# Linear attention and a gated feed-forward in one kernel: the weight fold moved to the front, output stores moved to another queue, and a new order of steps

## The chip, the cores and the metric

The kernel runs on one core of a Trainium2 chip. The metric is the device time of one execution in microseconds (us); lower is better. A core has a matrix engine (PE), a vector engine (DVE), a scalar engine (ACT), a general engine (POOL) and a synchronisation engine (SP). Each takes its instructions strictly in program order; they meet through semaphores. DMAs are issued from SP's queue (descriptors made in hardware) or POOL's (descriptors made by software), and are carried out by 16 DMA engines.

## The reference

With batch 8, 8 heads, 576 positions, head width 64, model width 512 and inner width 1024:

```python
phi = lambda x: np.where(x > 0, x, np.exp(x) - 1.0) + 1.0
q_p, k_p = phi(q), phi(k)
kv  = np.einsum('bhsd,bhse->bhde', k_p, v)
z   = np.sum(k_p, axis=2)
num = np.einsum('bhsd,bhde->bhse', q_p, kv)
den = np.einsum('bhsd,bhd->bhs', q_p, z)[..., None] + 1e-06
x   = (num / den).transpose(0, 2, 1, 3).reshape(4608, 512)
out = (((x @ w1) * (x @ w2)) @ w3) @ w_out
```

All inputs and the output are float32; the kernel multiplies in bf16 and accumulates in float32.

## The kernel before

Since `(h @ w3) @ w_out = h @ (w3 @ w_out)`, the kernel first multiplies the two weights into one, `wf` (1024 x 512): this is called the fold here. The 4608 tokens are cut into 36 tiles of 128 and 9 chunks of 512 columns. Of each batch, 512 positions make four tiles; the remaining 64 are joined with the 64 of the next batch to a ninth tile of the pair.

The whole kernel is one long list of steps, written out by hand in the string `ORDER`. A step has a letter, a batch or chunk, and a part; a `+` puts its copy on DVE instead of ACT (in a load: its DMA on POOL instead of SP). Every engine and every DMA queue does its share of the steps in this order, so a step that waits holds everything behind it on that engine or queue. The letters:

- `L`, `M`, `N`: load k, q, v of a batch (`load_qkv`; parts 0 and 1 are the halves by heads, 2 is all, 3 the 64 remaining positions). They land in a pool of five buffers (`ld`) that the raw w3 shares.
- `E0` to `E7`, `C0`, `C1`, `B0` to `B3`: load w3, w_out and the quarters of w1 and w2, on POOL's queue, with a cast from float32 to bf16 in the DMA.
- `X Y Z` for q and `x y z` for k: phi as exp (ACT), min and max (both DVE). `v`: v to bf16.
- `w`, `W`: fold of one of eight row blocks of w3. `w` is eight PE transposes and a copy, `W` eight matmuls and a copy.
- `c d e f g a b r`: attention of batch 0, with q transposed on PE (`first_tr`); `h`, `i`: the first two units of chunk 0.
- For other batches: `K` makes kv, `T` transposes q by a DMA, `A` makes numerator and denominator and divides, and x is transposed by a DMA (`D`) or on PE (`P`).
- `F c.f`: one of eight units of a chunk: 4 + 4 matmuls with w1 and w2, an ACT copy and a DVE product. `O c.m`: eight matmuls of one tile with `wf`, a copy into `o_sb`, and its store, issued in the same step: on POOL's queue, for the last chunk on SP's.

The fold's steps stand among those of chunk 0, after the attention of batch 0. The constants (identity, masks, ones) are written on POOL ahead of all steps. One explicit wait holds `B0`, and all that stands behind it on POOL's queue, until the second half of k of batch 0 has landed; another holds the load `M1.2` for `E5`.

Of the kernel before, what the change touches and what calls it, by code (L numbers as in the profile page):

```python
# [8 lines left out]
F32 = mybir.dt.float32  # L9
BF16 = mybir.dt.bfloat16  # L10
# [3 lines left out]
P = 128  # L14
NCH = 512
# [3 lines left out]
def kernel(  # L19
# [47 lines left out]


    ident = consts.tile([P, P], BF16)
    make_identity(nc, ident)  # L70

    mask = consts.tile([P, 2, 2, D], BF16)
    nc.gpsimd.memset(mask, 0.0)
    nc.gpsimd.memset(mask[0:D, :, 0, :], 1.0)
    nc.gpsimd.memset(mask[D:P, :, 1, :], 1.0)
    eps = consts.tile([P, 1], F32)
    nc.gpsimd.memset(eps, 1e-6)

    w1_sb = wpool.tile([P, KC, DFF], BF16)
    w2_sb = wpool.tile([P, KC, DFF], BF16)  # L80
# [71 lines left out]
    def copy_of(alt):  # L152
        return nc.vector.tensor_copy if alt else nc.scalar.copy
# [132 lines left out]

    kvz = {}

    def first_tr(g):
        qj, _ = ph["q", 0]  # L290
        if g == 0:
            qts[0, 0] = att.tile([P, KC, NJ * P], BF16, tag="qt", name="qt")
        tp = at_ps.tile([P, 8, P], BF16, tag="at", name="tp")
        for i in range(2):
            for j in range(NJ):
                nc.tensor.transpose(tp[:, i * NJ + j, :],
                                    qj[:, 2 * g + i, j].rearrange("p u d -> p (u d)"), ident)
# [11 lines left out]
    def first_nd(hp, own):  # L309
        if own:  # L310
            nd = [mm_ps.tile([P, 512], F32, tag="mm", name=n) for n in ("num1", "den1")]
        else:
            t = at_ps.tile([P, 2, 512], F32, tag="at", name="nd1")
            nd = [t[:, 0], t[:, 1]]
        g, a = divmod(hp, 2)
        for i, n in ((1, "z"), (0, "n")):
            nc.tensor.matmul(nd[i], kvz[n, g][:, a].rearrange("p h e -> p (h e)"),
                             qts[0, 0][:, hp], start=True, stop=True)
        r = lr.tile([P, 512], F32, tag="lr", name="lr", bufs=2)

        def recip():
            nc.scalar.activation(out=r, in_=nd[1], func=AF.Ln, bias=eps[:, 0:1])  # L322
            nc.scalar.activation(out=r, in_=r, func=AF.Exp, scale=-1.0)  # L323

        def mult():
            nc.vector.tensor_tensor(
                out=xt[:, 0:NJ, hp, :], in0=nd[0].rearrange("p (j t) -> p j t", t=P),
                in1=r.rearrange("p (j t) -> p j t", t=P), op=ALU.mult)
        return recip, mult

    def first_rest():
# [3 lines left out]
        for i, n in ((1, "z"), (0, "n")):  # L335
            for hp in range(KC):
# [1 line left out]
                nc.tensor.matmul(nd[:, i, hp * R:(hp + 1) * R],  # L338
                                 kvz[n, g][:, a].rearrange("p h e -> p (h e)"),
                                 qtr[:, a, g * R:(g + 1) * R], start=True, stop=True)  # L340
        r = lr.tile([P, 512], F32, tag="lr", name="lr", bufs=2)
        w = KC * R
        nc.scalar.activation(out=r[:, 0:w], in_=nd[:, 1, 0:w], func=AF.Ln, bias=eps[:, 0:1])
        nc.scalar.activation(out=r[:, 0:w], in_=r[:, 0:w], func=AF.Exp, scale=-1.0)
# [28 lines left out]
    def o_unit(c, m, alt=False):  # L373
        ab = abs_[c]
        o_ps = mm_ps.tile([P, DM], F32, tag="mm", name="o_ps")
        for f in range(FC):
            nc.tensor.matmul(o_ps, ab[:, f, m * P:(m + 1) * P], wf_sb[:, f, :],  # L377
                             start=(f == 0), stop=(f == FC - 1))
        o_sb = sm.tile([P, DM], F32, tag="o_sb", name="o_sb", bufs=4)
        copy_of(alt)(out=o_sb, in_=o_ps)  # L380
        kind, b, j = order[c * (NCH // P) + m]
        queue = nc.sync if c == n_chunks - 1 else nc.gpsimd
        if kind == "J":
            dst = out[b * S:b * S + NJ * P, :].rearrange("(p j) n -> p j n", j=NJ)
            queue.dma_start(out=dst[:, j, :], in_=o_sb)  # L385
        else:
            for i in range(2):
                queue.dma_start(
                    out=out[(b + i) * S + NJ * P:(b + i + 1) * S, :],
                    in_=o_sb[i * R:(i + 1) * R, :])  # L390


    WQ = 256
# [30 lines left out]
            nc.tensor.transpose(tp[:, kc, :], raw["w3", i][:, kc * P:(kc + 1) * P], ident)  # L424
# [39 lines left out]
    ctx.enter_context(tc.manual_schedule())
    src = {"k": k, "q": q, "v": v}
    held = {}
    GATE = 5

    def step(s):

# [6 lines left out]
            f_unit(b, i)  # L477
        elif t == "O":
            o_unit(b, i, alt)
        elif t == "w":  # L480
            w3_tr(b, alt)
        elif t == "W":
            wf_mm(b, alt)
        elif t in "LMN":
            name = "kqv"["LMN".index(t)]
            ins = load_qkv(name, src[name], b, i, alt)
            if b == 0:
                held[t, i] = ins
            if s == "M1.2":
                after(ins, held["E", GATE])  # L490
        elif t == "B":
            for ins in load_w12(b):
                if b == 0 and "B" not in held:
                    after(ins, held["L", 1])
                    held["B"] = True
        elif t == "C":
            load_wo(b)
        elif t == "E":
            held["E", b] = load_w3(b)
        elif t in "xX":  # L500
            phi_exp("kq"["xX".index(t)], b, i)
        elif t in "yY":
# [74 lines left out]
```

## Time and profile before

| What | Value |
|---|---|
| median of 3 runs | 267.1 us (266.4 to 267.88) |
| the profiled execution, its own time | 265.35 us |
| its span in the profile | 263.6 us |
| PE busy | 234.8 us (89%) |
| DVE / ACT / POOL busy | 165.2 / 129.4 / 42.8 us |
| moved by DMA | 50.55 MB, mean 192 GB/s |
| last PE work ends | about 258.8 us |

All positions in time below are microseconds from the start of the span. A row of a group gives the busy time, the mean time of one instruction in ns, and the idle time before them with what ended it. `SPq` is the queue on which SP issues DMAs. Matmul durations overlap their neighbours (they are pipelined), so what one costs is read from the distance of starts. L358 and the like are lines of the kernel before. The profiled execution is 1.75 us faster than the median of the runs, and its span is 1.75 us shorter than its own time.

### The profile page before, as it was taken

How to read it: one execution, taken by the hardware profiler on the slowest of the kernel's cores; microseconds unless marked ns; L12 is line 12 of the kernel's file. 1: busy time of each engine (PE TensorE's matmuls, PEld its weight loads, DVE VectorE, ACT ScalarE, POOL GpSimd, SP SyncE). 2: the span in 40 equal slices, each digit the busy share in tenths (PEclk: the TensorE clock that was granted, in tenths of full speed). 3: DMA queues.
4: the chain of work that ended last, by engine and by line, in shares of the span. 5: the costliest groups of instructions: out<-in, count | busy, mean ns of one | idle time of the engine just before them, and what ended most of it. 6: DMA issues, size and time to landing. Idle time of an engine off the chain costs nothing.

```text
span 263.6 us, 4384 instructions
## 1 busy us (share of the span) xinstructions
PE 234.8 (89%) x1591; PEld 112.2 (43%) x1608; DVE 165.2 (63%) x416; ACT 129.4 (49%) x207; POOL 42.8 (16%) x81
## 2 busy tenths in 40 slices
PE   0086999899599999995999999999999999999992
PEld 0043544454245545441544444444445444444440
DVE  0564352788668797695479886967985826442220
ACT  4465524793767693693463952624633213222211
POOL 4472500002300031030001500310110030001000
PEclk9999999999889999997999999999999999999998
DMA  6999999959999949799997994795634071011123
GB/s 234 324 180 204 212 226 321 334 111 270 281 235 269 350 139 260 224 259 277 236 338 152 216 379 95 228 160 191 145 93 133 2 178 31 20 42 50 71 88 111
DMA packets 73173, 50.55 MB, mean 192 GB/s; under 512 B 39616, under 2 KB 69312, under 8 KB 73152
## 3 DMA queue, kind: packets, MB, share of 16 engines
q1 hardware_dynamic: 63600, 35.59, 52.3%
q0 software_dynamic: 9552, 14.68, 23.7%
q8 instruction: 12, 0.20, 0.3%
q14 instruction: 9, 0.07, 0.1%
HBM read 38.80 MB, written 9.44 MB: 183 GB/s over the span
## 4 chain that ended last, share of the span: by engine, by line
PE 81%; DMA 8%; ACT 4%; DVE 3%; issue 1%; SPq 0%; POOL 0%; DVEq 0%
PE a_ps L358 25%; PE b_ps L358 24%; PE o_ps L377 19%; PE wf_ps L430 5%; DMA xt<-xn 3%; PE kvp L186 3%; DMA q32r<-in_q_dram 2%; DMA q<-in_q_dram 2%; PE nd L252 2%; PE w3p L424 1%; DVE qj L149 1%; ACT xt L273 1%; ACT o_sb L380 1%; ACT lr L322 0%; ACT lr L323 0%
## 5 line engine op out<-in xcount | busy, mean ns | idle before, releaser
L358 PEld LDWEIGHTS <-w_sb 128*128 128x128 bf16 x576 | 55.3, 99 | 69.9 <-issue 5.0
L364 DVE TENSOR_TENSOR ab<-a_sb,b_ps 128x512 bf16<-128x512 f32 x72 | 49.2, 684 | 50.4 <-PE b_ps L358 45.9
L358 PE MATMUL a_ps<-xt,w_sb 128*128 128x512 bf16 x288 | 76.8, 387 | 4.1 <-DMA xt<-xn 3.0
L363 ACT COPY a_sb<-a_ps 128x512 f32<-128x512 f32 x72 | 42.1, 586 | 73.1 <-PE a_ps L358 69.7
L358 PE MATMUL b_ps<-xt,w_sb 128*128 128x512 bf16 x288 | 76.5, 385 | 0.0
L377 PE MATMUL o_ps<-wf_sb,ab 128*128 128x512 bf16 x274 | 64.6, 379 | 1.1 <-issue 0.5
L385 POOL DMA_DIRECT2D out_dram<-o_sb x29 | 15.9, 548 | 172.9 <-ACT o_sb L380 129.6
L377 PEld LDWEIGHTS <-ab 128*128 128x128 bf16 x288 | 27.4, 98 | 31.9
L149 DVE SCALAR_TENSOR_TENSOR qj<-q,e 128x256 bf16<-128x256 f32 x64 | 23.6, 415 | 0.0
L149 DVE SCALAR_TENSOR_TENSOR kj<-k,e 128x256 bf16<-128x256 f32 x64 | 23.4, 414 | 0.1
L380 ACT COPY o_sb<-o_ps 128x512 f32<-128x512 f32 x23 | 13.4, 586 | 20.3 <-PE o_ps L377 18.3
L128 DVE TENSOR_SCALAR e<-e 128x1024 bf16<-128x1024 bf16 x32 | 13.0, 418 | 11.3 <-ACT e L124 11.3
L124 ACT ACTIVATE e<-q 128x1024 bf16<-128x1024 f32 x16 | 16.8, 1058 | 6.2 <-DMA q<-in_q_dram 6.2
L262 DVE TENSOR_TENSOR xn<-nd,r 128x512 bf16<-128x512 f32 x28 | 18.0, 685 | 0.0
L124 ACT ACTIVATE e<-k 128x1024 bf16<-128x1024 f32 x16 | 16.7, 1059 | 0.3 <-DMA k<-in_k_dram 0.3
L380 DVE COPY o_sb<-o_ps 128x512 f32<-128x512 f32 x13 | 9.0, 689 | 11.8 <-PE o_ps L377 10.8
L430 PE MATMUL wf_ps<-wo_sb,w3t 128*128 128x512 bf16 x61 | 14.6, 379 | 0.9 <-ACT w3t L425 0.7
L158 ACT CAST vt<-v 128x1024 bf16<-128x1024 f32 x14 | 14.6, 1053 | 0.8 <-DMA v<-in_v_dram 0.8
L206 PE MATMUL kvp<-vt,kj 128*128 128x130 bf16 x16 | 2.0, 264 | 13.0 <-ACT vt L158 13.0
L190 ACT COPY kvf<-kvp 128x260 f32<-128x260 f32 x14 | 5.3, 375 | 9.6 <-PE kvp L186 9.2
L430 PEld LDWEIGHTS <-w3t 128*128 128x128 bf16 x64 | 6.1, 98 | 7.8 <-ACT w3t L425 0.8
L186 PEld LDWEIGHTS <-kj 64*128 64x128 bf16 x224 | 7.1, 94 | 4.4 <-issue 3.2
(75 smaller groups left out, 157.4 us busy)
## 6 DMA issues: line engine op xcount, KB each, us to landing
out_dram<-o_sb POOLq DMA_DIRECT2D x29, 256.0 KB, 3.7
q<-in_q_dram SPq DMA_DIRECT2D x7, 1024.0 KB, 7.1
k<-in_k_dram SPq DMA_DIRECT2D x7, 1024.0 KB, 8.2
v<-in_v_dram SPq DMA_DIRECT2D x6, 1024.0 KB, 8.1
v<-in_v_dram SPq DMA_DIRECT2D x4, 512.0 KB, 7.1
w_sb<-in_moe_w_dram POOLq DMA_DIRECT2D x8, 256.0 KB, 9.0
w3b<-in_moe_w_dram POOLq DMA_DIRECT2D x8, 256.0 KB, 11.6
q<-in_q_dram SPq DMA_DIRECT2D x2, 512.0 KB, 5.1
```

What stands on the lines that cost most here:

```text
L124: nc.scalar.activation(out=e, in_=x, func=AF.Exp)
L149: nc.vector.scalar_tensor_tensor(out=out, in0=x, scalar=1.0, in1=e, op0=ALU.add, op1=ALU.max)
L158: copy_of(alt)(out=vt[:, :, 4 * i:4 * i + 4, 0:D], in_=raw["v", b].rearrange("p (h j d) -> p j h d", h=H, j=NJ)[:, :, 4 * i:4 * i + 4])
L186: nc.tensor.matmul(kvp[:, r, i * W:(i + 1) * W], kk[rows], vv[rows], start=(n == 0), stop=(n == (NJ if r == g else NJ - 1)))
L262: nc.vector.tensor_tensor(out=dst.rearrange("p (c u) e -> p u c e", u=2), in0=v4[:, :, :, 0:D], in1=r[0:n].unsqueeze(3).to_broadcast([n, 2 ...
L358: nc.tensor.matmul(ps, w[:, kc, f * P:(f + 1) * P], xt[:, 4 * c:4 * c + 4, kc, :], start=(kc == 0), stop=(kc == KC - 1))
L363: nc.scalar.copy(out=a_sb, in_=a_ps)
L364: nc.vector.tensor_mul(out=abs_[c][:, f, :], in0=a_sb, in1=b_ps)
L377: nc.tensor.matmul(o_ps, ab[:, f, m * P:(m + 1) * P], wf_sb[:, f, :], start=(f == 0), stop=(f == FC - 1))
L380: copy_of(alt)(out=o_sb, in_=o_ps)
L385: queue.dma_start(out=dst[:, j, :], in_=o_sb)
L430: nc.tensor.matmul(ps, w3ts[i][:, kc, :], wo_sb[:, kc, :], start=(kc == 0), stop=(kc == FC - 1))
```

## The change

- The list starts with `E0`, `C0`, `E1` on POOL; the constants become steps (`I`) behind them, and `w0`, `w1` are PE's first work. `U` is the first half of a fold product (w_out's first half suffices), `W` then the second. `H9` is nine matmuls on a tile of zeros.
- Explicit waits are a table: `L0.0` waits until `E0` has landed, `E4` for `N0.1`, `B0` for `L0.1`, `L1.2` for `C1`, `M1.2` for `E3`, `N1.0` for `E7`.
- All loads of q, k, v go on SP's queue (eight pairs of small ones were on POOL's).
- Stores are steps of their own (`S`), all on SP's queue; `o_sb` has five buffers instead of four.
- The last tile (`Q8.2`) is made in two column halves, one copied and stored by DVE and SP, the other by ACT and ACT's own queue. The tile with two DMAs is no longer the last.
- q of batches 1 and 2 is transposed on PE (`a`, `b`) instead of by DMA (`T`); x of batch 3 instead of batch 2 is transposed on PE (`P`), that of batch 2 by DMA (`D2.0`).
- The divisor's buffer in batch 0's attention comes from the three buffers of `a_sb`.
- The whole order is new.

```diff
     ident = consts.tile([P, P], BF16)
-    make_identity(nc, ident)
...
+    def constants(part):
+        if part == 0:
+            make_identity(nc, ident)
+        elif part == 1:
...
+        else:
+            nc.vector.memset(zero, 0.0)
+
+    def warm_up(n):
+        ps = mm_ps.tile([P, NCH], F32, tag="mm", name="warm")
+        for _ in range(n):
+            nc.tensor.matmul(ps, zero[:, 0:P], zero, start=True, stop=True)
...
-        r = lr.tile([P, 512], F32, tag="lr", name="lr", bufs=2)
+        r = sm.tile([P, NCH], F32, tag="a_sb", name="lr")
...
-        o_sb = sm.tile([P, DM], F32, tag="o_sb", name="o_sb", bufs=4)
+        o_sb = o_sbs[c, m] = sm.tile([P, DM], F32, tag="o_sb", name="o_sb", bufs=OBUF)
         copy_of(alt)(out=o_sb, in_=o_ps)
+
+    def o_store(c, m):
+        o_sb = o_sbs[c, m]
         kind, b, j = order[c * (NCH // P) + m]
-        queue = nc.sync if c == n_chunks - 1 else nc.gpsimd
...
-            queue.dma_start(out=dst[:, j, :], in_=o_sb)
+            nc.sync.dma_start(out=dst[:, j, :], in_=o_sb)
...
+    def o_last(c, m):
...
+        for i, copy, queue in ((0, nc.vector.tensor_copy, nc.sync), (1, nc.scalar.copy, nc.scalar)):
+            cols = slice(i * (DM // 2), (i + 1) * (DM // 2))
+            o_ps = mm_ps.tile([P, DM], F32, tag="mm", name="o_ps")[:, 0:DM // 2]
+            for f in range(FC):
+                nc.tensor.matmul(o_ps, ab[:, f, m * P:(m + 1) * P], wf_sb[:, f, cols],
+                                 start=(f == 0), stop=(f == FC - 1))
+            copy(out=o_sb[:, cols], in_=o_ps)
+            queue.dma_start(out=dst[:, j, cols], in_=o_sb[:, cols])
...
+        if part != 1:
+            wfs[i] = mm_ps.tile([P, DM], F32, tag="mm", name="wf_ps")
+        for kc in ((0, 1, 2, 3), (4, 5, 6, 7), range(FC))[part]:
+            nc.tensor.matmul(wfs[i], w3ts[i][:, kc, :], wo_sb[:, kc, :],
                              start=(kc == 0), stop=(kc == FC - 1))
-        copy_of(alt)(out=wf_sb[:, i, :], in_=ps)
+        if part:
+            copy_of(alt)(out=wf_sb[:, i, :], in_=wfs[i])
...
     ORDER = """
-    M0.0 L0.0 X0.0 Y0.0 M0.1 L0.3+ L0.1 x0.0 X0.1 Y0.1 N0.3 N0.0 Z0.0 v0.2 y0.0 v0.0 Z0.1 z0.0
-    Z0.2 B0 Z0.3 E0 x0.2 E1 N0.1 y0.2 x0.1 z0.1 z0.4 c0.0 a0.0 y0.1 v0.1 b0.0 z0.2 C0 d0.0 E2
...
+    L0.3 E0 I2 C0 M1.3 E1 I0 w0 L0.0 x0.2 x0.0 w1 y0.0 E2 I1 M0.0 C1 E3 y0.2 X0.0 M0.1 U0 Y0.0
+    N0.3 X0.1 Z0.0 H9 N0.0 Z0.1 Y0.1 w2+ N0.1 W0+ z0.0 N1.3 a0.0 U1 E4 E5 z0.1 b0.0 L0.1 Z0.2
+    v0.2+ W1 E6 w3 v0.0+ Z0.3 U2 z0.4 c0.0 x0.1 L1.2 X1.2 v0.1+ a0.1 d0.0 W2 E7 L1.3 b0.1 e0.0
+    y0.1 U3 w4 z0.2 B0 z0.3 f0.0 M1.2 N1.0 N1.1 Y1.2 x1.0 M2.2 c0.1 g0.0 x1.1 W3 y1.0 w5+ U4
+    e0.1 f0.1 U5 y1.1 M2.3 x1.2 d0.1 z1.0 g0.1 W4 w6 w7+ v1.2 y1.2 z1.1 W5 e0.2 X1.0 U6 Y1.0 B1
+    Z1.4 W6+ U7 Z1.0 Z1.1 f0.2 W7 g0.2 B2 e0.3 h0.0 B3 X1.1 f0.3 h0.1 z1.2 a1.0 L2.2 Y1.1 g0.3
+    Z1.2 M0.3 Z1.3 v1.0 z1.4 b1.0 h0.2 z1.3 h0.3 i0.0 K1.0 a1.1 i0.1 v1.1 L2.3 F0.2 K1.1+ b1.1
+    F0.3 L3.3 A1.0 N2.3 F0.4 X2.0 F0.5 X2.1 Y2.1 Y2.0 P1.0 A1.1 X2.2 P1.1 Y2.2 Z2.0 F0.6 N2.2
+    F0.7 T1.1 Z2.1 x2.0 X0.2 x2.1 Y0.2 Z2.4 O0.2 Z2.2 P1.3 P1.2 O0.1 y2.1 Z2.3 a2.0 y2.0 z2.0
+    z2.1 Z0.4 v2.1 x2.2 O0.0 L4.3 M3.2 b2.0+ y2.2 v2.0+ v2.2 F1.0 A1.2 z2.4 x3.2 z2.2 L3.2 F1.1
+    y3.2 F1.2 X3.0 K2.0+ X3.1 S0.1 z2.3 T0.1 Y3.0 F1.3 N3.2 S0.2 z3.4 a2.1 Z3.0 x4.2 Y3.1 b2.1
+    Z3.1 M3.3 K2.1+ F1.4 Z3.2 M4.2 x3.0 N3.3 F1.5 S0.0 Z3.3 D1.1 N4.3 x3.1 A2.0 F1.6 X3.2 F1.7
+    y4.2 O1.0 y3.0 A2.1 v3.2 z3.0 v3.1 X4.0 Y3.2 Y4.0 O1.2 z3.1 r0 z4.4 y3.1 T3.0 O1.1+ D2.0
+    Z4.0 X4.1 O1.3+ O0.3+ v3.0 Y4.1 L4.2 M5.3 M4.3 N5.3 N4.2 z3.2 z3.3 Z4.1 T2.1 L5.2 K3.0+ F2.0
+    F2.1 S1.1 K3.1+ F2.2 x4.0 Z4.2 F2.3 Z3.4 x4.1 A3.0 S1.2 F2.4 Z4.3 F2.5 X4.2 L5.3 A3.1 T3.1
+    M5.2 P3.0 F2.6 y4.0 Y4.2 P3.1+ P3.2 y4.1 Z4.4 N6.3 z4.0 X5.2 M6.3 z4.1 S0.3 F2.7 x5.0 F3.0
+    z4.2 T4.1 x5.2 v4.2+ v4.1 v4.0 S1.0 T4.0 F3.1 A3.2 x5.1 A2.2 F3.2 y5.1 O2.0 z4.3 N5.2 y5.0
+    F3.3 K4.0+ K4.1+ X5.0 L6.2 Y5.2 Y5.0 D2.1 O2.3 S1.3 z5.0 O2.2 A4.0 P3.3 F3.4 A4.1 z5.1 y5.2
+    Z5.4 F3.5 L6.3 F3.6 v5.2 X5.1 z5.2 z5.4 v5.0 Z5.0 v5.1 D3.1 Y5.1 F3.7 x6.2 x6.0 Z5.1 O2.1+
+    S2.3 D4.0 K5.0+ z5.3 x6.1 O3.1+ Z5.2 M6.2 Z5.3 S2.0 y6.0 F4.0 K5.1+ y6.1 O3.3+ F4.1 z6.0
+    S2.2 X6.0 T5.0 Y6.0 T5.1 F4.2 S3.1 X6.2 X6.1 F4.3 N6.2 Z6.0 F4.4 z6.1 Y6.2 A5.0 F4.5 F4.6
+    A5.1 y6.2 O3.2 L7.2 A4.2 F4.7 v6.0 x7.0 S2.1 v6.1 S3.3 D5.0 Y6.1 v6.2 O4.3 Z6.1 z6.4 A5.2
+    z6.2 Z6.4 S3.2 O4.0+ Z6.2 z6.3 L7.3 x7.2 y7.0 O3.0 M7.2 Z6.3 K6.0+ T6.0 F5.0 D4.1 F5.1 F5.2
+    N7.3 F5.3 N7.2 K6.1+ O4.2 X7.0 S4.3 X7.1 z7.0 A6.0 F5.4 Y7.0 F5.5 Y7.1 S3.0 x7.1 Z7.0 S4.2
+    M7.3 F5.6 D5.1 A6.1 S4.0 F5.7 v7.0 O5.1+ O4.1 Z7.1 v7.1 O5.0 O5.3 z7.1 Z7.2 X7.2 D6.0 y7.1
+    z7.2 Z7.3 y7.2 F6.0 F6.1 v7.2 z7.4 F6.2 T6.1 F6.3 A6.2 F6.4 S4.1 S5.3 T7.0 z7.3 K7.0+ S5.1
+    Y7.2 F6.5 Z7.4 K7.1+ O5.2 A7.0 F6.6 A7.1 S5.0 F6.7 O6.3 T7.1 O6.1+ A7.2 O6.2+ S5.2 D7.0 D6.1
+    O6.0 F7.0 F7.1 D7.1 F7.2 F7.3 F7.4 F7.5 F7.6 F7.7 S6.1 S6.2 O7.0+ S6.3 S7.0 F8.0 F8.1 F8.2
+    O7.2 F8.3 F8.4 F8.5 S6.0 S7.2 O7.1 S7.1 F8.6 F8.7 O7.3 O8.0 S8.0 O8.3+ S8.3 O8.1 S7.3 S8.1
+    Q8.2
     """
+    GATES = "B0<L0.1 E4<N0.1 L0.0<E0 L1.2<C1 M1.2<E3 N1.0<E7"
...
+    OBUF = 5
+
+    def loaded(s, ins):
+        s = s.rstrip("+")
+        if s in gates and gates[s] in held:
+            after(ins, held[gates[s]])
+            del gates[s]
+        held[s] = ins
```

## The prediction

> **What bounds the kernel now.** I read the page first: how much of the span is PE, and in which slices it is not.
>
> ```profile
> span 263.6 us, 4384 instructions
> PE 234.8 (89%) x1591; PEld 112.2 (43%) x1608; DVE 165.2 (63%) x416; ACT 129.4 (49%) x207; POOL 42.8 (16%) x81
> PE   0086999899599999995999999999999999999992
> DMA  6999999959999949799997994795634071011123
> PE 81%; DMA 8%; ACT 4%; DVE 3%; issue 1%; SPq 0%; POOL 0%; DVEq 0%
> ```
>
> PE carries 81% of the chain, and the slices (6.6 us each) show where it does not work: two at the start, one with 5 near 69 us, one near 122 us, and the tail. DMA is full through all of the first third. So I asked PE's waits, then the timeline at these places.
>
> ```profile
> PE kvp L206 <- ACT vt L158: 13.0, 1, 13.0
> PE a_ps L358 <- DMA xt<-xn: 3.0, 1, 3.0
> PE w3p L424 <- DVE xt L326: 1.7, 1, 1.7
> PE xtp L272 <- ACT o_sb L380: 1.6, 1, 1.6
> PE a_ps L358 <- ACT xt L273: 1.1, 1, 1.1
> ```
>
> The columns are total, times, longest. 13.0 us pass before the first matmul: q, k, v of batch 0 must land and go through phi first.
>
> ```profile
> 17.66 0.59 PE L317 MATMUL den<-qt,kvz 128*128 128x512 bf16 x1
> 18.04 0.63 PE L317 MATMUL num<-qt,kvn 128*128 128x512 bf16 x1
> 18.46 0.63 PE L317 MATMUL den<-qt,kvz 128*128 128x512 bf16 x1
> 22.07 0.38 PE L358 MATMUL b_ps<-xt,w_sb 128*128 128x512 bf16 x1
> 22.29 0.38 PE L358 MATMUL a_ps<-xt,w_sb 128*128 128x512 bf16 x1
> 69.78 1.21 PE L358 MATMUL a_ps<-xt,w_sb 128*128 128x512 bf16 x4 [1.14 <-ACT xt L273]
> 122.06 1.89 PE L358 MATMUL a_ps<-xt,w_sb 128*128 128x512 bf16 x4 [2.96 <-DMA xt<-xn]
> ```
>
> After a pause PE is slow: equal matmuls start 0.42 us apart at 18 us and 0.216 apart from 22 us. By such distances the cold start costs 2.1 us. At 69.78 the first sixteen matmuls take 5.3 us where 3.45 is normal, so 1.85 is lost; at 122.06 the first eight lose 1.66. The granted clock of the next view shows both places.
>
> ```profile
> 5.00:10.00 5.00, 0.00 (x0) 0.00 (x0) 1.20 (x4) 2.70 (x3) 0.00 (x0) 1.00 1.07 344
> 25.00:30.00 5.00, 4.49 (x37) 2.77 (x38) 2.15 (x4) 3.20 (x5) 2.26 (x4) 1.00 1.30 202
> 30.00:35.00 5.00, 5.00 (x31) 2.52 (x30) 2.42 (x5) 1.01 (x1) 1.81 (x3) 1.00 1.33 212
> 68.00:75.00 7.00, 5.85 (x29) 2.57 (x29) 3.53 (x10) 3.96 (x8) 2.10 (x4) 0.76 1.19 203
> 120.00:127.00 7.00, 4.94 (x31) 2.09 (x32) 3.50 (x10) 1.08 (x3) 0.54 (x1) 0.76 1.09 264
> ```
>
> The last three columns are clock, DMA share and GB/s. Plain loads run at 344 GB/s; while weights are cast it is about 207, counted in the bf16 bytes written, since the share is above 1 in both. These two rates price the new start.
>
> **The start.** PE's work is the same; what counts is how much of it is done by when. A fold block is eight transposes (0.45 us, from the starts 36.18 and 36.63) and eight matmuls at 0.216 (1.72): 17.4 us for eight. The attention of batch 0 before the first `h` is 4.2 us (`c` 1.6, `a` 0.9, `e` eight matmuls, 1.7). So 21.6 us of PE work stand before `h0.0` in the new order; `H9` is extra.
>
> When can it be done? w3 and w_out write 3.15 MB at 0.207 MB per us, 15.2 us; q, k, v of batch 0 without q's rest are 3.4 MB at 0.344, 9.9 us. First bytes flow at 2.3 us, so all that is in by 27.4, and by 30.5 if `L1.2` (1.05 MB, 3.05 us), free to go after `C1`, gets ahead. PE's queue has `w7` before `W5 e0.2 U6 W6 U7 W7 e0.3`: after E7 lands, 0.45 + 5.1 = 5.6 us remain. So `h0.0` starts near 36.1; its `B0` (0.52 MB, 2.5 us) is in by 33. The ends: 33.0 with E7 at 27.4; 41 if each POOL DMA lands as slowly as the median w3 row below, E7 then being in near 35.
>
> ```profile
> out_dram<-o_sb POOLq DMA_DIRECT2D x29, 256.0 KB, 3.7
> w3b<-in_moe_w_dram POOLq DMA_DIRECT2D x8, 256.0 KB, 11.6
> ```
>
> From `h0.0` to `F1.0` the new list has `h` 3.45, six F units 10.35, `a1` and `a2.0` 1.35, `K1` 1.2, `A1.0 A1.1` 0.85, eight transposes per pair of `P` 1.8 and three O units 5.2: 24.2 us, and I add 1.5 for waits like those that stand there now (0.7 on w3t, 1.1 on xt), bounds 0 to 4. `F1.0` starts near 61.8, against 69.8 now. Then it still owes `O0.3` and `A1.2` (2.0 us), which are done by now in the old order, so the lead is 6.0 us; `a2.1` takes 0.45 of it. If PE comes there without a pause, the 1.85 us of slow clock go too: 7.4. Bounds by the ends above: 11 and 0.
>
> `H9` is nine matmuls, 3.8 us at the cold distance. It stands between `U0` and `w2`, while E2 and C1 are still landing (C1 is the fourth or fifth transfer, at the rates above near 13 us), so it is in a wait and costs nothing; if they were in, it would cost 1.9 to 3.8, within the bound. What it buys is uncertain: the Trainium skill, TensorE: Matmul & The Clock Gate, section on the clock gate, says that the fast clock needs about 3.4 us of activity and is lost after an idle window as long; the trace shows the slow distance but not the window. By that rule a wait of that length behind `H9` makes the next matmuls cold again, at up to 2 us.
>
> The constants move behind three POOL DMAs. `ident` is needed by `w0`; three issues at 0.55 to 0.9 and 0.5 for the identity put it at 3.3 us, ahead of E0. `L0.0` waits for E0, and on SP all of q, k, v stands behind it. E0 is alone; the nearest rows are q's first load, read 3.8 us after issue, and w3's fastest, 6.2: E0 in near 6, and the loads already pay for this in the byte sum, since POOL's DMAs fill that time.
>
> **The middle.** The 4.6 us at 122 us (3.0 wait, 1.66 clock) come from `D3.0`, 8.3 us to landing. Batch 3 now goes through PE (0.45 each, ACT or DVE 0.6) with `F2.7` between, so this stall goes. Batch 2 takes the risk: `D2.0` follows `A2.1`. DVE needs 2.5 us after its matmuls (111.19 to 113.65 in the old trace), the transfer 4.3 (median) to 8.3, thus 6.8 to 10.8; PE has `O1.2 r0 O1.1 O1.3 O0.3 K3.0` there, 7.8 us. Stall 0 to 3.0, with slow clock 4.7. I take 1: gain 3.6, bounds 0 to 4.6.
>
> **The stores.** 35 DMAs leave POOL for SP, and 16 small loads too. SP's own store issues took 0.36 us, small loads 0.63: 23 us more of SP's queue, which is not full; two `T` at some 1.6 leave. POOL is not waited for by anyone in the middle, so nothing is gained there. But a store step waits for its copy, and behind it stand loads, `T` and `D`. Behind `S0.1` waits `T0.1`, behind `S0.0` `D1.1`, behind `S1.3` and `S2.3` `D3.1` and `D4.0`. Most `S` follow their `O` by several F units (1.73 us each), which is the cover. No row shows a store ahead of a transpose. The least is 0; the most is a stall as at 122 us, 4.6, at three places, 13.8. I take 2.5, nearer to none because of that distance. The rule against the change stands in the Trainium skill, DMA: Bandwidth & Descriptors, section "Queues, rings and completion order": a DMA engine takes turns between queue rows but consumes one row in order. By it a transpose queued behind a 256 KB store would land later by the store's bytes; the trace has no such pair. At 344 GB/s that is an estimated 0.76 us each, which the sum leaves out.
>
> **The tail.** Now: last matmul 258.8, ACT copy 0.59, two issues of 0.57, landing. Then: half a copy (0.3 less), one issue (0.57 less), but sixteen half-width matmuls instead of eight with their weight loads of 98 ns each nearly bare (up to 0.3 more). I take 0.5 less, 0 to 0.9. `lr` in `a_sb`'s buffers costs nothing while no F unit needs them, and these start after `e0.3`; a fifth `o_sb` only loosens.
>
> **Sum** against the profiled execution's own 265.35: -7.4 - 3.6 + 2.5 - 0.5 = -9.0, giving 256.35; the median of the runs is 1.75 above that execution, so 258.1.
>
> **Rivals.** (a) The start is bound by bytes and software DMAs as slow as the w3 row: `h0.0` at 41, lead 1 to 2. For: 11.6 us median landing, DMA full. Against: they were queued behind 3.4 MB and each other. Time 267.1 - 1.5 - 3.6 + 2.5 - 0.5 = 264. Chance 0.2. (b) Slower: SP's in-order queue becomes the bound. Mechanism: a store waiting for its copy holds a `T` or `D` of the next batch, at the places named. Price 4.6 each with the clock loss; with the other gains of 11.5 it breaks even between two and three such stalls, and at three the time is 267.1 - 11.5 + 13.8 = 269.4, more with four (274). For: SP waits already, 44 us in all for `D`'s inputs. Against: the distance of `S` behind `O`. Chance 0.15. (c) The fast end: no new wait, `D2.0` covered: 267.1 - 9 - 4.6 - 0.5 = 253. Chance 0.2. (d) The front does not do what it says: E0 lands late, near the 12.7 us that the slowest w3 DMA took, and holds q, k, v by its gate. Every load shifts by 6, the lead is gone, and with the store cost the time is near 267. Chance 0.05.
>
> **The numbers.** The forecast gets 0.4, 258.1; with (a) and (c) that is 0.8. The range 251 to 267.5 leaves out most of (b) and a little of the fast end. A difference below about 0.5%, 1.3 us, can't be told from none. Faster: 0.8 less a little of (a), plus part of (d): 0.8; within: 0.05; slower: 0.15.
>
> **What would show it.** Right: first matmul near 6 us, `h0.0` (first a_ps) at 33 to 41, `F1.0` at 58 to 66, no row "DMA xt<-xn" above 3 us, granted clock 1.00 at F1's start, fewer than three waits of SPq for o_sb that end a PE wait. Wrong: PE idle in two or more slices after 60 us, with the chain running through SPq or an xt transposed late; or a first a_ps beyond 42 us.

## The result, and the profile after

The changed kernel takes 268.59 us (median of 12 runs, 267.33 to 270.51), the kernel before 265.75 beside it (15 runs, 261.56 to 267.88). The ratio is 1.0225, with a 95% interval of 1.0179 to 1.0271: slower, where 258.1 and "faster" were forecast, and outside the range of 251 to 267.5. Executions of one and the same kernel lie up to 7.7 us apart, with a mean granted clock between 0.97 and 1.00, and the ratios leave slow ones out, so that the ratio is 1.0225 where the two medians alone would give 1.011. Positions in a profile are therefore compared with positions in another, ratios with ratios, and the profiled execution of a kernel may lie some us beside its median.

The same lines of the page as were shown for the kernel before, in the same order:

```profile
span 267.1 us, 4436 instructions
PE 239.0 (89%) x1630; PEld 115.8 (43%) x1649; DVE 164.4 (62%) x417; ACT 133.1 (50%) x211; POOL 14.1 (5%) x30
PE   1285945999999999999999999999999999999994
DMA  7998999996969749998959695879682144021115
PE 81%; DMA 12%; ACT 2%; issue 1%; DVE 1%; SPq 0%; ACTq 0%; POOLq 0%
```

The holes that PE had near 69 and 122 us are gone, and from the eighth slice to the last but one PE is full. Apart from the tail, nearly all of its idle time now lies in the first seven slices (46.7 us). The chain's DMA share rose from 8% to 12%. PE's waits, in total us, times and longest, name what is behind it:

```profile
PE w3p L454 <- DMA w3b<-in_moe_w_dram: 10.9, 2, 5.9
PE wf_ps L464 <- ACT wf_sb L467: 6.6, 1, 6.6
PE tp L309 <- DVE qj L162: 3.9, 1, 3.9
PE kvp L223 <- DVE kr L162: 0.9, 2, 0.4
PE wf_ps L464 <- issue: 0.4, 2, 0.2
PE o_ps L390 <- issue: 0.3, 2, 0.2
```

That is the whole list. Nothing above 0.5 us comes from the middle: no transposed x is waited for, and no store. Rows of PE's timeline give the places that the prediction named, the first `a_ps` (`h0.0`) and `F1.0`, and the wait of 6.6 us ahead of them:

```profile
5.05 1.03 PE L454 MATMUL w3p<-ident,w3b 128*128 128x128 bf16 x8 [5.05 <-DMA w3b<-in_moe_w_dram]
11.98 1.03 PE L454 MATMUL w3p<-ident,w3b 128*128 128x128 bf16 x8 [5.90 <-DMA w3b<-in_moe_w_dram]
22.84 1.28 PE L309 MATMUL tp<-ident,qj 128*128 128x128 bf16 x8 [3.94 <-DVE qj L162]
42.94 3.57 PE L464 MATMUL wf_ps<-wo_sb,w3t 128*128 128x512 bf16 x8 [6.61 <-ACT wf_sb L467]
52.51 0.38 PE L371 MATMUL a_ps<-xt,w_sb 128*128 128x512 bf16 x1
77.20 1.03 PE L371 MATMUL a_ps<-xt,w_sb 128*128 128x512 bf16 x4
```

`h0.0` starts at 52.51 instead of the forecast 36.1, and `F1.0` at 77.20 instead of 61.8 (before: 69.78). From `F1.0` to the end of the span it is 189.9 us, against 193.8 before, although the new order still owes 2.45 us of work there. So everything behind `F1.0` gained and the start lost more.

The wait of 6.6 us names ACT's copy `wf_sb`. ACT's timeline shows that this copy takes 0.57 us and was not itself the trouble:

```profile
34.46 0.63 ACT L336 ACTIVATE lr<-lr 128x512 f32<-128x512 f32 x1
40.41 2.00 ACT L137 ACTIVATE e<-k 128x1024 bf16<-128x1024 f32 x2 [5.33 <-DMA k<-in_k_dram]
42.32 0.57 ACT L467 CAST wf_sb<-wf_ps 128x512 bf16<-128x512 f32 x1
```

ACT stood from 35.1 to 40.4 before `x1.0`, the exp of batch 1's k, whose load had not landed. The copy of `W3` stands behind it in the order, and PE needs the PSUM tile that this copy frees. The chain of waits says why the load was late (start, length, what):

```profile
5.49 14.96 DMA q<-in_q_dram
...
24.34 2.54 PE wf_ps L464 x7
27.35 12.98 DMA k<-in_k_dram
40.41 2.00 ACT e L137 x2
42.94 3.57 PE wf_ps L464 x8
```

Rows of the waits of POOL, and then of SP's queue, complete it, with the row of SP's timeline where the load `N1.0` is issued:

```profile
POOL w3b L445 <- DMA v<-in_v_dram: 18.8, 1, 18.8
```

```profile
SPq L120 <- PE w3p L454: 5.0, 1, 5.0
SPq L120 <- DMA w3b<-in_moe_w_dram: 3.7, 2, 2.2
```

```profile
36.01 5.67 SPq L120 DMA_DIRECT2D v<-in_v_dram  x2
```

SP's load `L1.2` takes the next of the five `ld` buffers, which the raw w3 shares; it waits 5.0 us until PE has transposed an earlier block (`w3`), and that stands in PE's queue behind `a0.0`, which waits for q of batch 0. POOL meanwhile idles 18.8 us at the gate `E4<N0.1`, until 25.4. The longest wait for w3, 2.2 us, ends at 36.0: there `N1.0` is released by its gate, so E7 has landed. From 1.2 to 13 us the DMAs are busy all the time but move only 170 GB/s; between 24 and 28 us they have little under way; and behind the 6.6 us PE runs at half clock (columns: length, busy time and count of PE, PEld, DVE, ACT, POOL, then granted clock, DMA share, GB/s):

```profile
1.20:13.00 11.80, 2.05 (x17) 1.76 (x18) 0.00 (x0) 2.15 (x3) 5.13 (x14) 1.00 1.01 170
24.00:28.00 4.00, 3.78 (x21) 1.80 (x20) 4.00 (x11) 2.10 (x3) 2.60 (x5) 0.74 0.63 151
40.00:46.00 6.00, 3.06 (x8) 1.20 (x9) 3.36 (x8) 4.00 (x6) 0.00 (x0) 0.50 1.26 247
68.00:75.00 7.00, 6.95 (x39) 3.39 (x38) 7.00 (x23) 5.64 (x11) 0.00 (x0) 1.00 1.11 355
120.00:127.00 7.00, 6.95 (x47) 3.19 (x46) 6.17 (x18) 5.69 (x9) 0.00 (x0) 1.00 0.91 172
```

The last two rows answer to the two of before that had a clock of 0.76: both are at 1.00 now.

### The profile page after: what moved, and what is told of

It reads as the page before. It is cut to its first block, busy times and chain, and to the rows that moved or that the text cites. A ratio compares the mean times of both kernels' runs of the same rounds, so it can differ in the third digit from the quotient of the medians.

```text
span 267.1 us, 4436 instructions
## 1 busy us (share of the span) xinstructions
PE 239.0 (89%) x1630; PEld 115.8 (43%) x1649; DVE 164.4 (62%) x417; ACT 133.1 (50%) x211; POOL 14.1 (5%) x30
## 4 chain that ended last, share of the span: by engine, by line
PE 81%; DMA 12%; ACT 2%; issue 1%; DVE 1%; SPq 0%; ACTq 0%; POOLq 0%
PE a_ps L371 23%; PE b_ps L371 23%; PE o_ps L390 23%; DMA q<-in_q_dram 6%; DMA k<-in_k_dram 5%; PE wf_ps L464 4%; PE kvp L199 3%; PE nd L265 2%; ACT e L137 2%; DMA w3b<-in_moe_w_dram 1%; DVE qj L162 1%; PE xtp L285 1%; PE tp L309 1%; PE o_ps L417 1%; PE w3p L454 1%
## 5 line engine op out<-in xcount | busy, mean ns | idle before, releaser
L371 PEld LDWEIGHTS <-w_sb 128*128 128x128 bf16 x576 | 54.4, 98 | 63.6 <-issue 0.4
L371 PE MATMUL a_ps<-xt,w_sb 128*128 128x512 bf16 x288 | 75.1, 380 | 0.1
L371 PE MATMUL b_ps<-xt,w_sb 128*128 128x512 bf16 x288 | 74.9, 379 | 0.0
L390 PE MATMUL o_ps<-wf_sb,ab 128*128 128x512 bf16 x264 | 63.1, 379 | 1.0 <-issue 0.3
L390 PEld LDWEIGHTS <-ab 128*128 128x128 bf16 x280 | 26.5, 98 | 30.9
L464 PE MATMUL wf_ps<-wo_sb,w3t 128*128 128x512 bf16 x61 | 18.6, 445 | 7.2 <-ACT wf_sb L467 6.6
L454 PE MATMUL w3p<-ident,w3b 128*128 128x128 bf16 x64 | 5.7, 245 | 10.9 <-DMA w3b<-in_moe_w_dram 10.9
L171 ACT CAST vt<-v 128x1024 bf16<-128x1024 f32 x13 | 13.4, 1046 | 0.0
L454 PEld LDWEIGHTS <-w3b 128*128 128x128 bf16 x64 | 4.8, 111 | 12.7 <-DMA w3b<-in_moe_w_dram 11.2
L199 PE MATMUL kvp<-vt,kj 64*128 64x130 bf16 x208 | 8.7, 218 | 0.0
```

What stands on the lines that cost most here:

```text
L171: copy_of(alt)(out=vt[:, :, 4 * i:4 * i + 4, 0:D], in_=raw["v", b].rearrange("p (h j d) -> p j h d", h=H, j=NJ)[:, :, 4 * i:4 * i + 4])
L199: nc.tensor.matmul(kvp[:, r, i * W:(i + 1) * W], kk[rows], vv[rows], start=(n == 0), stop=(n == (NJ if r == g else NJ - 1)))
L371: nc.tensor.matmul(ps, w[:, kc, f * P:(f + 1) * P], xt[:, 4 * c:4 * c + 4, kc, :], start=(kc == 0), stop=(kc == KC - 1))
L464: nc.tensor.matmul(wfs[i], w3ts[i][:, kc, :], wo_sb[:, kc, :], start=(kc == 0), stop=(kc == FC - 1))
```

## The experiments

Theory 1: the start is late because waits on loads hold whole queues: the gates `L0.0<E0` and `E4<N0.1`, the buffer that `L1.2` waits for, and ACT's order, in which a step of batch 1 stands ahead of the fold's copies. The rest of the new order is better than the old. Theory 2 (rival b of the prediction): SP's queue, with stores and small loads on it, is what costs. Theory 3 (rival a): the start is bound by bytes, whatever the order.

All twelve, with the ratio to the kernel before; span, first `a_ps`, `F1.0` and what follows `F1.0` are of the profiled execution, in us:

| run | ratio (95%) | span | first `a_ps` | `F1.0` | rest |
|---|---|---|---|---|---|
| the change | 1.0225 (1.0179 to 1.0271) | 267.1 | 52.51 | 77.20 | 189.9 |
| e1 old start, new rest | 0.9887 (0.9832 to 0.9942) | 260.9 | - | 70.76 | 190.1 |
| e2 stores on POOL | 1.0216 (1.0165 to 1.0266) | 268.3 | 51.71 | 76.40 | 191.9 |
| e3 batch 1's phi later | 1.0262 (1.0211 to 1.0313) | 270.0 | 45.27 | 80.09 | 189.9 |
| e4 `L1` before `E4` | 0.9858 (0.9804 to 0.9912) | 263.5 | 48.88 | 73.57 | 189.9 |
| e5 no gate `L0.0<E0` | 1.0085 (1.0034 to 1.0135) | 263.4 | 48.86 | 73.55 | 189.9 |
| e6 no gate `E4<N0.1` | 1.0091 (1.0042 to 1.014) | 263.5 | 49.00 | 73.69 | 189.8 |
| e7 `B1` after `M1.2` | 1.0142 (1.01 to 1.0183) | 265.4 | 50.80 | 75.50 | 189.9 |
| e8 three together | 0.9869 (0.9786 to 0.9951) | 260.7 | 44.24 | 70.89 | 189.8 |
| e9 old start, junction mended | 0.9856 (0.9794 to 0.9918) | 259.5 | - | 68.76 | 190.7 |
| e10 e4 without gate `L0.0<E0` | 0.9876 (0.98 to 0.9953) | 258.5 | 43.90 | 68.59 | 189.9 |
| e11 no warm-up | 1.0196 (1.0134 to 1.0259) | 267.8 | 53.20 | 77.89 | 189.9 |
| e12 small loads later | 0.9844 (0.9727 to 0.9961) | 260.8 | 46.13 | 70.83 | 190.0 |

The last column is the first finding: whatever is done to the start, the rest takes 189.8 to 190.1 us. It differs only where the rest itself was edited (e2, e9).

**e1: the old start, the new rest.** The old order up to `F1.0`, with the old gates and the constants first; then those steps of the new order that are not done yet. Twelve of these still stand ahead of `F1.0`, among them `a2.0` and `b2.0+`.

```diff
-    L0.3 E0 I2 C0 M1.3 E1 I0 w0 L0.0 ... O0.0 L4.3 M3.2 b2.0+ y2.2 v2.0+ v2.2 F1.0 A1.2 ...
+    I2 I0 I1 (the old order up to F1.0) x2.1 ... a2.0 ... b2.0+ v2.0+ v2.2 F1.0 (the new order's remaining steps)
-    GATES = "B0<L0.1 E4<N0.1 L0.0<E0 L1.2<C1 M1.2<E3 N1.0<E7"
+    GATES = "B0<L0.1 M1.2<E5"
```

> The old order up to F1.0 (old gates, constants first, no U and no H9), then the new order from there with its S steps on SP's queue, Q8.2 and five o_sb buffers. Theory 1 (the loss is all in the new start, the new rest is faster and the stores on SP cost nothing): F1.0 starts at 69 to 71 as in the kernel before, PE has no wait above 1 us after it, and the time is 258 to 261, some 5 to 7 below the kernel before. Theory 2 (stores and all loads on SP's in-order queue cost time): the rest is not faster, PE waits on xt or on nd appear after 75 us, time 265 or more.

Measured: ratio 0.9887, median 262.06. With the same rest as the changed kernel and only the start of before, the ratio falls by 3.3%: the loss is in the start. As far as the stores go, Theory 2 has no room for that, since all of them are still on SP. For the small loads e1 settles nothing, since four pairs of the start (`L0.3 L1.3 M2.3 N2.3`) are back on POOL here. PE's timeline at the junction shows what is left (four matmuls are 0.87 us apart at full clock):

```profile
68.85 0.40 PE L309 MATMUL tp<-ident,qj 128*128 128x128 bf16 x4 [0.89 <-DVE qj L162]
70.53 0.40 PE L309 MATMUL tp<-ident,qj 128*128 128x128 bf16 x4 [1.28 <-DVE qj L162]
70.76 1.24 PE L371 MATMUL a_ps<-xt,w_sb 128*128 128x512 bf16 x4
71.79 1.91 PE L371 MATMUL b_ps<-xt,w_sb 128*128 128x512 bf16 x4
73.50 1.70 PE L371 MATMUL a_ps<-xt,w_sb 128*128 128x512 bf16 x4
```

**e2: the stores back on POOL.**

```diff
     def o_store(c, m):
...
-            nc.sync.dma_start(out=dst[:, j, :], in_=o_sb)
+            nc.gpsimd.dma_start(out=dst[:, j, :], in_=o_sb)
```

> The changed kernel with only the S steps' DMAs issued on POOL's queue instead of SP's (Q8.2 stays). Theory 1: within 1 us of the changed kernel, 267.5 to 269.5. Theory 2: the stores on SP are the loss, 262 to 265.

Measured: ratio 1.0216, the same. From `F1.0` to the last PE work it is 186.0 us in both kernels, so the stores on SP cost nothing in the middle. SP does wait for copies (27.7 us in six waits for ACT's `o_sb`, 14.6 in one for DVE's), but no wait of PE follows. Only the tail differs: the last PE work ends at 262.4 and the span at 268.3, thus 5.9 us against 3.9. Theory 2 falls for the stores.

**e3: phi of batch 1 later on ACT.** `x1.0 y1.0 x1.1 y1.1 z1.0 z1.1 X1.0 Y1.0 Z1.0 Z1.1 x1.2 y1.2` are taken out of the fold's steps.

```diff
-    h0.0 B3 X1.1 f0.3 h0.1 ...
+    h0.0 B3 X1.1 f0.3 x1.0 y1.0 x1.1 y1.1 z1.0 z1.1 X1.0 Y1.0 Z1.0 Z1.1 x1.2 y1.2 h0.1 ...
```

> The changed kernel with phi of batch 1 (x1.0 x1.1 x1.2 X1.0 and the y, z, Y, Z that hang on them) moved behind f0.3, so that ACT no longer stands before the load of k of batch 1 while the fold's copies queue behind it. Theory 1a (ACT's in-order wait for L1.2 holds the fold): PE's wait of 6.6 us at 36 goes, the first a_ps moves from 52.5 to 45 to 48, time 262 to 265. Theory 3 (the start is bound by the bytes, whatever the order): the wait only changes its name, first a_ps at 50 to 52, time 267 to 270.

Measured: the first `a_ps` at 45.27, as Theory 1 said, and the 6.6 us are gone; but the time did not fall (1.0262). `X1.1`, also of batch 1, was left ahead of `f0.3`, and q of batch 1 landed as late as before. PE's timeline:

```profile
55.93 1.28 PE L309 MATMUL tp<-ident,qj 128*128 128x128 bf16 x8 [8.76 <-DVE qj L162]
```

The wait moved from the fold to `a1.0`, one load further. Not all of the 8.76 us is the load's: q of batch 1 was in at 48.75, and its exp `X1.0` ran at 52.85, behind the steps that the new place put ahead of it, so an estimated 4.1 us (the difference) are e3's own order. ACT's order is where the late load reached PE, but the load is late in either order.

**e4: `L1.2` before the second half of w3.** The load then takes a free buffer, and `E4` to `E7` take those that come free.

```diff
-    z0.0 N1.3 a0.0 U1 E4 E5 z0.1 b0.0 L0.1 Z0.2 v0.2+ W1 E6 w3 v0.0+ ... c0.0 x0.1 L1.2 X1.2 ... W2 E7
+    z0.0 N1.3 L0.1 L1.2 a0.0 U1 z0.1 b0.0 Z0.2 v0.2+ W1 w3 E4 E5 E6 E7 v0.0+ ... c0.0 x0.1 X1.2 ... W2
```

> The changed kernel with L0.1 and L1.2 ahead of E4 to E7 in the list and E4 to E7 behind w3, so that L1.2 takes the fifth ld buffer, which is free, instead of waiting for the transposes of w3 to free E0's. E4 to E7 take E0's buffer instead, and issue about 2 us later. Theory 1b (the path to ACT's wait runs through L1.2's buffer): L1.2 issues by 23 instead of 27.4, lands by 36 instead of 40.3, first a_ps 3 to 5 us earlier than 52.5, time 264 to 266. Theory 3 (bytes): no change, 268 to 269.

Measured: ratio 0.9858, faster than the kernel before, and 3.6% below the change; in the profiled execution, the slowest of its five, `F1.0` moves by 3.6 us only. ACT no longer stands before `x1.0`, and the hole in the DMAs is closed (ACT's timeline, then the window):

```profile
35.19 0.63 ACT L336 ACTIVATE lr<-lr 128x512 f32<-128x512 f32 x1
35.72 1.99 ACT L137 ACTIVATE e<-k 128x1024 bf16<-128x1024 f32 x2
37.61 0.56 ACT L467 CAST wf_sb<-wf_ps 128x512 bf16<-128x512 f32 x1
```

```profile
24.00:28.00 4.00, 3.72 (x16) 1.86 (x18) 4.00 (x12) 1.28 (x2) 0.00 (x0) 0.61 1.02 343
```

343 GB/s against 151 in the same four us: the engines had not been the limit there, the order was. That speaks against Theory 3.

**e5 and e6: one gate less each.**

```diff
-    GATES = "B0<L0.1 E4<N0.1 L0.0<E0 L1.2<C1 M1.2<E3 N1.0<E7"
+    GATES = "B0<L0.1 E4<N0.1 L1.2<C1 M1.2<E3 N1.0<E7"          (e5)
+    GATES = "B0<L0.1 L0.0<E0 L1.2<C1 M1.2<E3 N1.0<E7"          (e6)
```

> The changed kernel with the wait of L0.0 for E0 taken out, so that k, q, v of batch 0 start with the first weights. Theory 1 (the start hangs on a chain of waits: q of batch 0 late, so w3's transposes late, so L1.2 late, so ACT's copies late): q lands 3 to 4 us before 20.5, first a_ps 2 to 4 us before 52.5, time 265 to 267; w0 a little later than 5.05. Theory 3 (bytes): whatever the first loads gain the weights lose, 268 to 269.

> The changed kernel with the wait of E4 for N0.1 taken out, so that POOL issues E4 to E7 at 6.6 us instead of 25.4. Theory 1: the DMA engines have no half-empty stretch at 24 to 34 us any more, but E4 to E7 (5 us at the rate of casts) now delay q of batch 0, L0.1 and L1.2, on which the chain hangs; first a_ps between 2 us earlier and 3 us later, time 266 to 271. A rival (the empty stretch alone is the loss): first a_ps 4 to 5 us earlier, time 263 to 265.

Measured: 1.0085 and 1.0091, `F1.0` 3.65 and 3.5 us earlier in the profiled executions. For e6 that execution is an ordinary one: 265.30 us, where its ten runs have a median of 265.80, 2.8 below the changed kernel's. For e5 it is the fastest of ten, by 2.0 us; the median of the ten is 268.53, next to 268.59 for the changed kernel, so its ratio is more than its runs bear out. Nor is q of batch 0 clearly in earlier without the gate, where 3 to 4 us were expected: its first exp starts at 19.05 in e5, and, with the gate in place and the same loads up to there, at 19.08 in e7, 19.43 in e2, 19.84 in e11, 20.47 in the changed kernel and 20.62 in e3. The rows of e5 and e7:

```profile
19.05 1.06 ACT L137 ACTIVATE e<-q 128x1024 bf16<-128x1024 f32 x1 [0.35 <-DMA q<-in_q_dram]
19.08 1.06 ACT L137 ACTIVATE e<-q 128x1024 bf16<-128x1024 f32 x1 [0.57 <-DMA q<-in_q_dram]
```

So the gate `E4<N0.1` has a price; that `L0.0<E0` has one is not shown. e6 also shows what its gate was good for: with w3's second half in flight beside q and k, PE's wait for q's phi grows from 3.9 to 7.2 us, while the one for `wf_sb` falls from 6.6 to 1.2.

**e7: the second quarter of w1 and w2 behind `M1.2`.** One gate more.

```diff
-    GATES = "B0<L0.1 E4<N0.1 L0.0<E0 L1.2<C1 M1.2<E3 N1.0<E7"
+    GATES = "B0<L0.1 E4<N0.1 L0.0<E0 L1.2<C1 M1.2<E3 N1.0<E7 B1<M1.2"
```

> The changed kernel with one wait more: B1, and B2 and B3 behind it on POOL's queue, wait until q of batch 1 (M1.2) has landed. If the 13 and 16 to 19 us to landing of k and q of batch 1 come from eight casts of w1 and w2 that are issued in one burst beside them: L1.2 lands by 36 to 38 instead of 40.3, M1.2 by 40 to 43 instead of 48, PE's wait of 6.6 us shrinks to 2 to 4, first a_ps at 48 to 50, time 263 to 266. If the order of the bytes does not matter (theory 3): 268 to 269.

Measured: 1.0142, `F1.0` 1.7 us earlier; `x1.0` at 39.03 instead of 40.41, later than expected. That need not be the gate's doing: q of batch 0 was 1.4 us earlier too in this execution, before the gate holds anything, and e2, without it, has `x1.0` at 39.44. What the gate does move is q of batch 1, as expected: it is in by 42.4 instead of 48.5, so the casts of w1 and w2 do slow a load beside them. The time gains little by it.

**e8: e4, no gate `L0.0<E0`, and `B1<M1.2`.**

> E4's edit (L0.1 and L1.2 ahead of E4 to E7, E4 to E7 behind w3) with both the wait of L0.0 for E0 taken out and B1 waiting for M1.2. Theory 1: first a_ps at 43 to 46, time 255 to 259, below both kernels. Theory 3 (bytes): 260 or more, no better than e4_L1_before_E4 alone (260.9).

Measured: the first `a_ps` at 44.24, as expected; the ratio is 0.9869, a smaller gain than expected, and PE now waits 1.7 us for `w_sb`, which `B1` loads; e10, the same kernel without `B1`'s gate, has no such wait. The gains don't add up.

**e9: e1 with the junction mended.** `a2.0` and `b2.0` go behind units that cover DVE's products.

```diff
-    ... a2.0 ... b2.0+ ... F1.0 ... F1.1 ...
+    ... F1.0 a2.0 ... F1.1 b2.0+ ...
```

> e1 with one joint mended: a2.0 behind F1.0 and b2.0 behind F1.1, so that PE does not stand 2.2 us before q of batch 2 and does not start F1 with the slow clock. Theory 1: F1.0 starts at 68 to 69.5 instead of 70.8, sixteen matmuls there in 3.5 us instead of 5.1, time 257.5 to 259.5, below every kernel so far. Theory 2 (the rest with stores on SP is no faster than the old rest): 262 or more.

Measured: 0.9856, median 260.45, some 1 us above what was expected. `F1.0` is now 1.0 us ahead of the kernel before, at full clock:

```profile
68.76 1.02 PE L371 MATMUL a_ps<-xt,w_sb 128*128 128x512 bf16 x4 [0.69 <-ACT xt L286]
69.62 1.03 PE L371 MATMUL b_ps<-xt,w_sb 128*128 128x512 bf16 x4
```

**e10: e4 without the gate `L0.0<E0`.**

> e8 without B1's wait. Theory 1: the wait of 1.7 us on w_sb goes, F1.0 at 69 to 71.5, and since the span has been F1.0 plus 189.9 in every run with the new start, span 259 to 261.5, time 260.5 to 263. Theory 3 (bytes): w_sb's casts delay q of batch 1 again by as much, F1.0 at 73 or later, time 265 or more.

Measured: span 258.5, `F1.0` at 68.59: the profiled execution, the fastest of its four (260.36 to 265.84), is 8.6 us shorter than that of the change, by one move in the order and one gate less. The ratio of 0.9876 can't be told from that of e4, so no gain of the second edit is shown here either. The load `N1.0`, which waits for E7, is issued at 35.07 instead of 36.01:

```profile
35.07 0.92 SPq L120 DMA_DIRECT2D v<-in_v_dram  x2
```

**e11: no `H9`.**

> The changed kernel without H9. If it stands in a wait, as the prediction had it: F1.0 at 76 to 78.5, time within 1.5 us of the changed kernel (267 to 270). If it holds w2 back: up to 2.8 us less.

Measured: 1.0196, `F1.0` 0.7 us later: the warm-up buys nothing that can be measured. A later window of the changed kernel shows why: PE waits 3.9 us for q's phi, and comes out of it slow; the mean granted clock of the window is 0.58.

```profile
22.00:26.00 4.00, 2.88 (x12) 1.49 (x14) 3.98 (x11) 2.07 (x2) 0.60 (x2) 0.58 0.80 236
```

**e12: e10 with the small loads of batch 1 further behind.** `M1.3 N1.3` behind `L1.2`, `X1.2` behind `f0.0`.

> e10 with M1.3 and N1.3 (four small loads of batch 1, which the old kernel had elsewhere or on POOL's queue) moved behind L1.2 on SP's queue, and X1.2 behind f0.1's first half on ACT accordingly. What is left of theory 2 (small loads on SP's in-order queue hold the start): k, q, v of batch 0 issue up to 3 us earlier, F1.0 at 66 to 67.5 instead of 68.6, time 258 to 259.5. Theory 1 (the transfers themselves share the DMA engines; SP's issue time is only their back-pressure): F1.0 at 68 to 70, 260 to 262.

Measured: `F1.0` at 70.83 instead of 68.59, the ratio 0.9844, which can't be told from e10's. Moving these two pairs gains nothing that the runs show (the interval is 1.2% to each side); `L0.3` and `N0.3` stayed where they were. Stronger against Theory 2 is that e4 and e10, with every small load still on SP, are as fast as e9, where four pairs of the start are on POOL.

e4, e8, e9, e10 and e12 beat both kernels by ratios between 0.9844 and 0.9876, and their intervals overlap widely; which of them is best is not settled. e9 has the old start and the others the new one, mended: even then no lead of the new start over the old is shown, and what these kernels gain on the kernel before is gained mostly behind `F1.0`, where they need some 190 us and that kernel 193.8.

## Why the prediction was wrong

Its structure held: lead at `F1.0`, middle, stores, tail. In its own terms, from the profiled spans (263.6 and 267.1, +3.5):

- **The start: forecast -7.4 (-11 to 0), measured +8.0.** `F1.0` at 77.20 is 7.4 later than 69.78; the 2.0 us still owed make a lead of -9.4, and with 0.45 for `a2.1` and 1.85 for the slow clock that is gone, +8.0. This is the step that failed, and with 15.4 us it is more than the whole miss. (The fast end of the range was mis-added: by the ends that it names, it is 12.0 and not 11. And read by starts, as the rest of the sum is, the slow clock at 69.78 cost 1.69 us and not 1.85, that at 122.06 1.59 and not 1.66; neither changes the picture.) The step has two parts, before and after the landing of E7.
  - **The byte sum: E7 in at 36.0, forecast 30.5 (27.4 to 35): 5.5 us.** The sum let the DMAs run at 207 and 344 GB/s from 2.3 us on without a pause. From 1.2 to 13 us they moved 170 GB/s at a share of 1.01: busy, but below both rates. From 24 to 28 us they moved 151 at a share of 0.63: there they paused, behind the gate `E4<N0.1`, which the prediction did not price at all and which costs 3.5 us in e6, and behind the buffer that `L1.2` waited for. The gate `L0.0<E0` was charged at nothing because "POOL's DMAs fill that time"; e5 and e10 don't show that this was wrong.
  - **"After E7 lands 5.6 us remain": measured 16.5, thus 10.9 more.** The prediction followed PE's queue only. It did not follow ACT's, in which `x1.0` and `x1.1` stand ahead of W3's copy, nor the five `ld` buffers, which chain `L1.2` to w3's transposes and so to q of batch 0. The 6.6 us wait and the 1.84 us of half clock behind it (3.57 for eight matmuls instead of 1.73) are 8.4 of the 10.9. In e10, where `L1.2` is issued early and ACT no longer waits for it, E7's landing at 35.1 is followed by 8.8 us. e4 and e3 show the cause: an earlier load removes the wait, another order on ACT passes it on to the next late load.
- **From `h0.0` to `F1.0`: forecast 25.7, measured 24.7.** Right. So were the first matmul ("near 6", 5.05) and the clock of 1.00 at `F1.0`.
- **`H9` costs nothing: right; that it may buy nothing: right,** by e11. The Trainium skill, TensorE: Matmul & The Clock Gate, "What's actually happening", puts the idle window after which the clock halves at some 3.4 us; the wait of 3.9 us with 0.58 behind it agrees. Other rows here needed less: the clock also fell behind a wait of 2.96 us (122.06 in the kernel before) and behind two of 0.89 and 1.28 close together (e1), so a wait need not be that long.
- **The middle: forecast -3.6, measured -3.6** (+3.5, less the start's 8.0 and the tail's -0.9, with the stores at 0 by e2). This is what is left over when the other terms are taken off, and that it fits to 0.1 is partly luck: the stall of 4.6 us at 122 us is gone and `D2.0`, charged with 1, does not stall, so 1.0 us more was lost behind `F1.0` than any row names.
- **The stores: forecast +2.5 (0 to 13.8), measured 0** in the middle, the low end. The rule cited against the change, on one row taken in order (the Trainium skill, DMA: Bandwidth & Descriptors, "Queues, rings and completion order"), would have made each transpose later by an estimated 0.76 us; no wait of PE shows it.
- **The tail: forecast -0.5, measured -0.9** (3.9 us from the last PE work to the end, 4.8 before). With the stores on POOL (e2) it is 5.9, so the gain hangs on their queue.

Of the rivals, (b) had the sign and nearly the time (269.4), by a mechanism that did not happen: no wait of PE stands behind a store, and e2, without the stores on SP, is no faster. (a), "the start is bound by bytes and software DMAs", named the right place with 0.2, and put `h0.0` at 41 at the latest; but it too had no waits between queues, and 264 came out of it. The prediction's own sign for being wrong, a first `a_ps` beyond 42 us, is what happened.

Open: between e10's first `a_ps` of 43.9 and the forecast 36.1 lie 7.8 us, 4.6 of them in E7's landing. The low rate from 1.2 to 13 us is there in e4, e10 and e12 as well (169, 166, 177 GB/s), so neither the gate `L0.0<E0` nor the small loads of batch 1 explain it. That casts and plain loads in flight at once move fewer bytes is only argued, and was not tried there.

## What to carry to other kernels

When work is moved to the front of a kernel, sum its bytes only after following each load to its start: what buffer it takes, who frees that, and what stands ahead of it on its queue; a byte sum is a lower bound and no forecast. Follow every in-order engine, not the busiest alone: here an activation for the next batch held the copy that the busiest engine needed, and the trace of waits names the copy, not the load behind it. A wait at a start is best mended at the load, since a step moved out of the way can pass the wait on to the next late load (e3).

## What the runs showed of the hardware

- Beside casting DMAs a plain load lands late: q's two 512 KB loads of batch 0 took a median of 15.4 us from issue to landing, and the 1 MB load of k 12.98; w_sb's casts took 18.0. In the kernel before, where plain loads went first, the two loads of q took a median of 5.1 (the slower one 6.3). That the casts do this is shown for one load: with six of w_sb's casts held back (e7), q of batch 1 was in by 42.4 us instead of 48.5.
- A 256 KB store issued by POOL takes 0.54 to 0.58 us of its queue (e2), by SP 0.33 to 1.42, median 0.52 (the changed kernel). With the stores on POOL the end comes 2.0 us later behind the last PE work, though no DMA moves anything in the last 3 us of e2's span; the cause is open.
- The kernel before, unchanged, had spans of 262.4 us at a mean granted clock of 0.998 and of 265.4 at 0.980, on one chip. What sets this apart from execution to execution is not shown.
